# Moving the closing copies, joins and one low part at the end of each 512-token chunk

## The chip, the cores and the metric

One core of a Trainium2 chip runs the whole program in one launch. The metric is the device time of one execution in microseconds (us). In the text PE is the matmul engine, PEld its weight loads, DVE the vector engine, ACT the scalar engine, POOL GpSimd, and SP the queue that issues most DMAs. Every engine takes its instructions in the order in which the program wrote them.

## The reference

The input `x` has 4 x 3008 tokens of 256 values. The first half mixes along the sequence: a real FFT, a complex 256 x 256 product with bias, a soft threshold, and the inverse FFT. The second half is a feed-forward layer over the 12032 resulting tokens, and the change lies in it alone:

```
h = x @ w_in                                     # 256 -> 2048
g = max(h, 0) + alpha * min(h, 0)
out = g @ w_out                                  # 2048 -> 256
```

All matrices are float32. The kernel splits each operand into a rounded high part and a low rest, and a product of two operands is three matmuls: high by high, high by low, low by high.

## The kernel before, in words

Up to about 690 us the kernel does the transforms and the feed-forward layer of the first 4480 tokens. The other 7552 tokens go through it in chunks of 512 (`SC`): 14 whole ones and a last one of 384 (`NS2` is 15). This stage is the loop over `k` at the end of `fft_mix_moe`, line 1207.

The 2048 hidden values of a chunk are made in 8 **pairs** (`PR`) of two blocks of 128. One round of the loop handles pair `k`:

- `s_l1` (line 781) issues 12 matmuls of 512 columns (line 791), 6 for each of the two blocks, into PSUM tiles `ps_h`, of which there are two. For each block ACT takes the negative part (line 794) and DVE finishes the activation into `sq` (line 795). With that the `ps_h` bank is free for the next pair.
- `s_l2` (line 874) runs the second layer for the pair two rounds earlier (`SLAG` is 2), 21 matmuls of 256 columns (lines 888 to 890). It uses Strassen's scheme in Winograd's form: seven products in place of eight. The first product goes to `o_last`, the next two to a tile `c`, two to `a`, two to `b`.
- `s_sums` (line 799) makes the seven operands out of `sq`. ACT: the high part `dh` of three blocks (line 810), the high parts `h13` (821) and `h24` (824) of the sums. DVE: the sums `t13` (816) and the two halves of `t24` (818, 820), the low parts `dl` (819) and `l13` (825). POOL: the low part `l24` (826). `h24` needs the second half of `t24`, and as ACT works in order, line 794 of the next pair comes behind `h24`.

The lines of the DVE for one pair are therefore, in order, 795 twice, 816, 818, 819, 820, 825; those of ACT 794 twice, 810, 821, 824.

When the eighth pair of a chunk has gone through `s_l2`, its output lies in four PSUM pieces and must be joined. That is in the round of the second pair of the next chunk, `k` = 9, 17, ..., 113. It is called **E** here, the rounds after it E+1 to E+7, and the eight rounds from one E to the next a **period**. In E, `s_copy` (line 903) lets ACT copy four pieces into SBUF (line 909), between `h13` and `h24`. Then `s_out` (line 912) starts: it is a generator, and each `next` lets it go one step. Three joins on DVE (line 921) come at the end of E, behind `l13`; one more in each of E+1 to E+4; then `turn(1)` in E+5 and `turn(0)` in E+7, each of which transposes half of the chunk with two DVE instructions (line 927) and leaves up to 12 DMAs for the SP queue, which are issued by `put` in the round after. In E+1 the first product of the new chunk goes to `o_last`, so it needs the copy of `o_last` to be over, and the products for `a` and `b` need the copies and joins that read the old `a` and `b`.

In some rounds the loop also rebuilds 376 tokens from the transform: 16 matmuls (line 617), copies on ACT (line 654) and low parts on DVE (line 656). Of the 13 periods from the first E (`k` = 9) to the last (`k` = 113), 9 have one such group and 4 have two.

In the last chunk (`z_parts`, `z_l2`) the sums aren't formed; there the second layer is plain, and its 384 tokens are stored at the very end by lines 858 and 860 and three DMAs on SP.

The order around a chunk's end is written out by hand in these lines of the loop:

```
s_sums(*spairs[k], None if last else ends)
if ends is not None:
    ending = s_out(ends)
    next(ending)
```

Of the kernel before, what the change touches and what calls it, by code (L numbers as in the profile page):

```python
# [9 lines left out]
F32 = mybir.dt.float32  # L10
# [5 lines left out]
AF = mybir.ActivationFunctionType  # L16
ALU = mybir.AluOpType
# [76 lines left out]
def fft_mix_moe(ctx, tc, x, w_r, w_i, b_r, b_i, w_in, w_out, alpha, la, rb, lc, rd, lf, cf, sel, out):  # L94
# [25 lines left out]
    NS2 = -(-(B * S - T0) // SC)  # L120
# [4 lines left out]
    work = ctx.enter_context(tc.tile_pool(name="work", bufs=2))  # L125
# [5 lines left out]
    V, G, A, PE = nc.vector, nc.gpsimd, nc.scalar, nc.tensor  # L131

    def f(t):
        return t.bitcast(F32)
# [199 lines left out]
    def put(*queues):  # L334
        for n, (o, i) in enumerate(stores):
            (queues or (nc.sync,))[n % max(len(queues), 1)].dma_start(out=o, in_=i)
        stores.clear()
# [42 lines left out]
    pa, pb, pm, p1, pc = {}, {}, {}, {}, {}  # L380
# [296 lines left out]
    o_last = ps_o.tile([128, 2, C], F32, tag="ol", name="o_last", bufs=1)  # L677
# [62 lines left out]
    HS = SC // 2  # L740
# [36 lines left out]


    sg, sa, sq = {}, {}, {}

    def s_l1(n, t):
        yh, yl = yt[CC + n]
        w1 = SC if n < NS2 - 1 else ZC
        q = work.tile([128, 2, SC], F32, tag="xt", name="sq")[:, :, 0:w1]
        for j in range(2):
            m = 2 * t + j
            ps = ps_h.tile([128, SC], F32, tag="h", name="ps_h")[:, 0:w1]
            k = 0
            for ct in range(CT):
                for w, a in ((0, yh), (0, yl), (1, yh)):  # L790
                    PE.matmul(ps, wi_h[m // FH][:, w, ct, 128 * (m % FH):128 * (m % FH) + 128], a[:, ct, 0:w1],  # L791
                              start=(k == 0), stop=(k == 3 * CT - 1))
                    k += 1
            A.activation(out=q[:, j], in_=ps, func=AF.Relu, scale=-1.0)  # L794
            V.scalar_tensor_tensor(out=q[:, j], in0=q[:, j], scalar=beta_s[:, m:m + 1], in1=ps,  # L795
                                   op0=ALU.mult, op1=ALU.add)
        sq[n, t] = q

    def s_sums(n, t, ends=None):
        q = sq.pop((n, t))  # L800
        if n == NS2 - 1:
            z_parts(t, q)
            return
        q = q.rearrange("p j n -> p (j n)")
        b12, b11, b22, b21 = (q[:, HS * k:HS * k + HS] for k in range(4))
        dh = work.tile([128, 3 * HS], F32R, tag="Xh", name="dh")
        dl = work.tile([128, 3 * HS], F32R, tag="Xl", name="dl")
        h13 = work.tile([128, 2, HS], F32R, tag="xh", name="h13")
        l13 = work.tile([128, 2, HS], F32R, tag="Yh", name="l13")
        A.activation(out=dh, in_=q[:, HS:], func=AF.Copy)  # L810
        d = [(dh[:, HS * k:HS * k + HS], dl[:, HS * k:HS * k + HS]) for k in range(3)]
        t13 = work.tile([128, 2, HS], F32, tag="zst", name="t13", bufs=3)
        t24 = work.tile([128, 2, HS], F32, tag="bt", name="t24", bufs=3)
        h24 = work.tile([128, 2, HS], F32R, tag="xl", name="h24")
        l24 = work.tile([128, 2, HS], F32R, tag="Yl", name="l24")
        V.tensor_tensor(out=t13, in0=q[:, HS:3 * HS].rearrange("p (k n) -> p k n", k=2),  # L816
                        in1=b12.unsqueeze(1).to_broadcast([128, 2, HS]), op=ALU.subtract)
        V.tensor_tensor(out=t24[:, 0], in0=b22, in1=t13[:, 0], op=ALU.add)
        V.tensor_tensor(out=dl, in0=q[:, HS:], in1=f(dh), op=ALU.subtract)  # L819
        V.tensor_tensor(out=t24[:, 1], in0=b21, in1=t24[:, 0], op=ALU.subtract)  # L820
        A.activation(out=h13, in_=t13, func=AF.Copy)
        if ends is not None:
            s_copy(ends)
        A.activation(out=h24, in_=t24, func=AF.Copy)  # L824
        V.tensor_tensor(out=l13, in0=t13, in1=f(h13), op=ALU.subtract)
        G.tensor_tensor(out=l24, in0=t24, in1=f(h24), op=ALU.subtract)  # L826
        sg[n, t] = d + [(h[:, k], l[:, k]) for h, l in ((h13, l13), (h24, l24)) for k in range(2)]

    def z_parts(t, q):
        g = []  # L830
        for j, tags in enumerate((("xh", "Yh"), ("xl", "Yl"))):
            hi, lo = (work.tile([128, SC], F32R, tag=tag, name="zg")[:, 0:ZC] for tag in tags)
            A.activation(out=hi, in_=q[:, j], func=AF.Copy)
            (V if j else G).tensor_tensor(out=lo, in0=q[:, j], in1=f(hi), op=ALU.subtract)
            g.append((hi, lo))
        sg[NS2 - 1, t] = g
# [59 lines left out]
             (block(0, 0), b11, a[:, 0], r, False), (block(1, 0), b21, a[:, 1], False, z),  # L896
             (s4, b22, b[:, 0], r, False), (s3, t3, b[:, 1], False, z)])

    so = {}

    se = {}

    def s_copy(n):

        a, b, c = sa[n]
        se[n] = []
        for p in (a[:, 0], c[:, 1], o_last[:, 0], b[:, 0]):
            t = work.tile([128, HS], F32, tag="gl", name="se", bufs=4)
            A.activation(out=t, in_=p, func=AF.Copy)
            se[n].append(t)  # L910

    def s_out(n):

        a, b, c = sa.pop(n)
        p1, p5, p4, p3 = se.pop(n)
        u2, u3, u4 = (work.tile([128, HS], F32, tag="gh", name="su", bufs=4) for _ in range(3))
        c1 = work.tile([128, 2, HS], F32, tag="Yt", name="c1", bufs=1)
        c2 = work.tile([128, 2, HS], F32, tag="Yc", name="c2", bufs=1)

        def join(o, x, y, op=ALU.add):  # L920
            V.tensor_tensor(out=o, in0=x, in1=y, op=op)

        def turn(k):
            pool, tag = ((const, "bias"), (work, "os"))[k]
            o = pool.tile([128, HS // 32, 32, 2], F32, tag=tag, name="oT", bufs=1)
            for h, src in enumerate((c1, c2)):
                V.transpose(out=o[:, :, :, h], in_=src[:, k].rearrange("p (b c) -> p b c", c=32))
            s_store(T0 + SC * n + HS * k, o)

        join(u2, c[:, 0], p1)  # L930
        join(c1[:, 1], a[:, 1], p1)
        join(u3, b[:, 1], u2)
        yield
        join(c2[:, 1], u3, p4)
        yield
        join(u4, u2, p5, ALU.subtract)
        yield
        join(c1[:, 0], u4, p3)
        yield
        join(c2[:, 0], u3, p5, ALU.subtract)  # L940
        yield
        turn(1)
        yield
        yield
        turn(0)
        yield

    def s_store(s0, o):

        rows = out.rearrange("(b p r) c -> b p r c", b=B, r=R)  # L950
        for k in range(HS // 128):
            n, end = s0 // CH + 32 * k, s0 // CH + 32 * k + 32
            j = 0
            while n < end:
                dg, p = divmod(n, NP)
                w = min(NP - p, end - n)
                g = dg % NCH
                for ci in range(4):
                    src = o[32 * ci + j:32 * ci + j + w, 4 * k:4 * k + 4].rearrange("p i c h -> p i (c h)")
                    stores.append((rows[dg // NCH][p:p + w, CH * g:CH * g + CH, 64 * ci:64 * ci + 64], src))  # L960
                n += w
                j += w
# [33 lines left out]
    with tc.manual_schedule():  # L996
# [151 lines left out]
        spairs = [(n, t) for n in range(NS2) for t in range(PR)]  # L1148
# [33 lines left out]
        def do(when, i):  # L1182
            for fn, args in when.pop(i, ()):
                fn(*args)
# [21 lines left out]
        ending = None  # L1206
        for k in range(len(spairs) + SLAG):
            ends = None
            do(pre, k)
            if k < len(spairs):  # L1210
                s_l1(*spairs[k])
            do(post, k)
            put()
            if k < SLAG:
                l2(NS - 2 + 2 * k)
            if k == 1:
                do(todo, NS - 1)
            if k >= SLAG:
                n, t = spairs[k - SLAG]
                if n == NS2 - 1:  # L1220
                    z_l2(t)
                else:
                    s_l2(n, t)
                    ends = n if t == PR - 1 else None
            if ending is not None:
                next(ending, None)
            if k < len(spairs):
                last = spairs[k][0] == NS2 - 1
                if last and ends is not None:
                    s_copy(ends)  # L1230
                s_sums(*spairs[k], None if last else ends)
            if ends is not None:
                ending = s_out(ends)
                next(ending)
        assert not pre and not post
        put(nc.scalar, nc.sync)
        assert not todo and not mid
# [30 lines left out]
```

## Time and profile before

| | |
|---|---|
| median of 3 runs | 1353.62 us (1352.44 to 1354.51) |
| time of the profiled execution | 1354.4 us |
| its span, first to last instruction | 1352.6 us |
| PE busy | 1333.0 us, 99% |
| DVE busy | 1047.4 us, 77% |
| ACT busy | 775.7 us, 57% |
| POOL busy | 396.6 us, 29% |
| granted clock of PE | 0.999 |

A busy share is an average over the whole span. PE's matmuls are pipelined and their ends are modelled, so that a short wait of PE can be missing from its busy time; the starts of its weight loads show it. In timelines a row gives the start in us from the start of the span, the duration, the engine, the line, the operation, and what it was waiting for in square brackets. Rows that follow each other with one line and one tile are merged, with their count behind the x.

### The profile page before, as it was taken

Reading aid. Unit: us, or ns where it says so; the run is one execution under the profiler, and the core shown is the slowest. Engines: PE = TensorE matmul, PEld = TensorE weight load, DVE = VectorE, ACT = ScalarE, POOL = GpSimd, SP = SyncE. Lnnn points to the kernel's source line nnn. Section 1 sums busy time; section 2 is a strip of 40 time slices with the busy share of each in tenths; the row PEclk is TensorE's granted clock in tenths of the full one; section 3 lists DMA queues with packets and bytes.
Section 4 is the critical chain, followed back from the end, with each engine's and each line's share of the span. In section 5 each row is a group of like instructions: output and inputs, shape, how many; then the busy total and the mean of one; then the engine's idle time right before and its main releaser. Section 6 shows DMA issues by size and latency. Waiting matters only on the chain.

```text
span 1352.6 us, 25212 instructions
## 1 busy us (share of the span) xinstructions
PE 1333.0 (99%) x9158; PEld 1244.5 (92%) x9158; DVE 1047.4 (77%) x1962; ACT 775.7 (57%) x1555; POOL 396.6 (29%) x417
## 2 busy tenths in 40 slices
PE   8999999999999999999999999999999999999997
PEld 4979999999999999999999999899899888998897
DVE  2767856777777777776678888888888888888884
ACT  3566655665566645555556566656665656566653
POOL 3964742222222222222222222222221222222221
PEclk9999999999999999999999999999999999999999
DMA  9974223342333312111110011100010001000101
GB/s 234 248 199 146 80 94 105 110 135 71 98 115 110 115 50 79 55 57 40 36 36 1 11 32 26 40 12 24 23 40 14 23 20 40 17 21 20 28 17 28
DMA packets 88119, 89.66 MB, mean 66 GB/s; under 512 B 42317, under 2 KB 70448, under 8 KB 87995
## 3 DMA queue, kind: packets, MB, share of 16 engines
q1 hardware_dynamic: 79700, 77.02, 20.2%
q0 software_dynamic: 5168, 8.02, 2.3%
q10 hardware_dynamic: 3127, 3.01, 0.7%
q8 instruction: 72, 1.18, 0.4%
q14 instruction: 52, 0.43, 0.1%
HBM read 50.49 MB, written 34.34 MB: 63 GB/s over the span
## 4 chain that ended last, share of the span: by engine, by line
PE 73%; DVE 12%; issue 7%; DMA 3%; ACT 3%; POOL 1%; SPq 1%; ACTq 0%; DVEq 0%; POOLq 0%
PE ps_h L791 15%; PE ps_h L686 13%; PE ps_m L488 6%; PE ps_o L888 4%; PE ps_o L890 4%; PE ps_o L889 4%; PE ps_d L617 3%; DVE sq L795 3%; PE ps_o L725 3%; PE ps_o L724 3%; PE ps_o L723 3%; PE ps_b L428 2%; DVE t L816 2%; PE o_last L724 1%; PE o_last L725 1%
## 5 line engine op out<-in xcount | busy, mean ns | idle before, releaser
L791 PE MATMUL ps_h<-yh,w 128*128 128x512 f32 (+1 forms) x960 | 315.0, 389 | 0.0
L826 POOL TENSOR_TENSOR l<-t,h 128x512 fp32r<-128x512 f32 x112 | 145.0, 1295 | 478.9 <-ACT h L824 465.8
L795 DVE SCALAR_TENSOR_TENSOR sq<-sq,beta_s,ps_h 128x512 f32<-128x512 f32 (+1 forms) x240 | 167.5, 735 | 57.6 <-ACT sq L794 57.0
L791 PEld LDWEIGHTS ps_h<-yh,w 128*128 128x128 f32 x960 | 179.9, 188 | 32.3 <-DVE sq L795 0.2
L686 PE MATMUL ps_h<-yh,w 128*128 128x384 f32 (+1 forms) x704 | 206.8, 336 | 0.9 <-DVE q L693 0.9
L791 PE MATMUL ps_h<-yl,w 128*128 128x512 f32 (+1 forms) x480 | 185.7, 387 | 0.0
L697 ACT ACTIVATE gh<-q 128x384 fp32r<-128x384 f32 (+1 forms) x192 | 99.1, 516 | 144.5 <-DVE q L693 143.4
L693 DVE SCALAR_TENSOR_TENSOR q<-q,beta_s,ps_h 128x384 f32<-128x384 f32 (+1 forms) x192 | 115.5, 601 | 85.3 <-ACT q L692 83.8
L698 POOL TENSOR_TENSOR gl<-q,gh 128x384 fp32r<-128x384 f32 (+1 forms) x90 | 96.6, 1074 | 263.0 <-ACT gh L697 256.2
L810 ACT ACTIVATE dh<-sq 128x768 fp32r<-128x768 f32 x112 | 94.9, 848 | 118.2 <-DVE sq L795 65.3
L794 ACT ACTIVATE sq<-ps_h 128x512 f32<-128x512 f32 (+1 forms) x240 | 129.0, 585 | 9.2 <-PE ps_h L791 6.4
L686 PEld LDWEIGHTS ps_h<-yh,w 128*128 128x128 f32 x704 | 129.3, 189 | 3.8 <-issue 0.8
L824 ACT ACTIVATE h<-t 128x512 fp32r<-128x512 f32 x112 | 70.9, 633 | 107.1 <-DVE t L820 107.1
L686 PE MATMUL ps_h<-yl,w 128*128 128x384 f32 (+1 forms) x352 | 116.5, 331 | 0.0
L692 ACT ACTIVATE q<-ps_h 128x384 f32<-128x384 f32 (+1 forms) x192 | 91.7, 478 | 42.7 <-PE ps_h L686 41.2
L725 PE MATMUL ps_o<-w,gl 128*128 128x256 f32 x384 | 108.0, 281 | 1.7 <-POOL gl L698 1.7
L724 PE MATMUL ps_o<-w,gh 128*128 128x256 f32 x384 | 107.8, 281 | 0.0
L723 PE MATMUL ps_o<-w,gh 128*128 128x256 f32 x384 | 107.7, 280 | 0.0
L819 DVE TENSOR_TENSOR dl<-sq,dh 128x768 fp32r<-128x768 f32 x112 | 106.7, 953 | 0.3
L791 PEld LDWEIGHTS ps_h<-yl,w 128*128 128x128 f32 x480 | 90.2, 188 | 13.6
L888 PE MATMUL ps_o<-h,sw_a 128*128 128x256 f32 x336 | 94.2, 280 | 0.0
L890 PE MATMUL ps_o<-l,sw_a 128*128 128x256 f32 x336 | 93.0, 277 | 0.0
(195 smaller groups left out, 3590.1 us busy)
## 6 DMA issues: line engine op xcount, KB each, us to landing
zt<-zd SPq DMA_DIRECT2D x32, 384.0 KB
zd<-zst SPq DMA_DIRECT2D x37, 256.0 KB
ad<-ast SPq DMA_DIRECT2D x48, 192.0 KB
bt<-ad SPq DMA_DIRECT2D x72, 128.0 KB
xt<-in_x SPq DMA_DIRECT2D x21, 320.0 KB
out<-oT SPq DMA_DIRECT2D x152, 32.0 KB
cw_s<-in_moe_w_in SPq DMA_DIRECT2D x8, 512.0 KB
cw_s<-in_moe_w_out SPq DMA_DIRECT2D x8, 512.0 KB
```

What stands on the lines that cost most here:

```text
L686: PE.matmul(ps, wi_h[m // FH][:, w, ct, 128 * (m % FH):128 * (m % FH) + 128], a[:, ct, 0:n], start=(k == 0), stop=(k == 3 * CT - 1))
L693: V.scalar_tensor_tensor(out=q, in0=q, scalar=beta_s[:, m:m + 1], in1=ps, op0=ALU.mult, op1=ALU.add)
L723: PE.matmul(a, hi[:, t], w[:, 0], start=(i, k) in first, stop=False)
L724: PE.matmul(a, hi[:, t], w[:, 1], start=False, stop=False)
L725: PE.matmul(a, lo[:, t], w[:, 0], start=False, stop=(i, k) in last)
L791: PE.matmul(ps, wi_h[m // FH][:, w, ct, 128 * (m % FH):128 * (m % FH) + 128], a[:, ct, 0:w1], start=(k == 0), stop=(k == 3 * CT - 1))
L794: A.activation(out=q[:, j], in_=ps, func=AF.Relu, scale=-1.0)
L795: V.scalar_tensor_tensor(out=q[:, j], in0=q[:, j], scalar=beta_s[:, m:m + 1], in1=ps, op0=ALU.mult, op1=ALU.add)
L819: V.tensor_tensor(out=dl, in0=q[:, HS:], in1=f(dh), op=ALU.subtract)
L826: G.tensor_tensor(out=l24, in0=t24, in1=f(h24), op=ALU.subtract)
L888: PE.matmul(o, wh, gh, start=first, stop=False)
L890: PE.matmul(o, wh, gl, start=False, stop=last)
```

## The change

At E, two copies (`o_last` and the first half of `a`) go ahead of `dh` on ACT; two joins go between the first half of `t24` and `dl` on DVE; the other two copies go behind `h13`, and the third join goes behind `dl`, ahead of the second half of `t24`. `l13` of that pair is issued a round later, ahead of the sums of E+1. The further steps of `s_out` are: nothing in E+1, a join in E+2, `turn(1)` in E+3, a join in E+4, two joins in E+5, nothing in E+6, `turn(0)` in E+7. At the last end (`k` = 113) the four copies and three joins are issued in one go ahead of that pair's parts, the fourth join follows in the next round, `turn(1)` and three joins in the round after, `turn(0)` in the third round; before, the same steps took seven rounds.

```diff
 def s_sums(n, t, ends=None):
...
         l13 = work.tile([128, 2, HS], F32R, tag="Yh", name="l13")
+        if ends is not None:
+            next(ends)
         A.activation(out=dh, in_=q[:, HS:], func=AF.Copy)
...
         V.tensor_tensor(out=t24[:, 0], in0=b22, in1=t13[:, 0], op=ALU.add)
+        if ends is not None:
+            next(ends)
         V.tensor_tensor(out=dl, in0=q[:, HS:], in1=f(dh), op=ALU.subtract)
-        V.tensor_tensor(out=t24[:, 1], in0=b21, in1=t24[:, 0], op=ALU.subtract)
         A.activation(out=h13, in_=t13, func=AF.Copy)
         if ends is not None:
-            s_copy(ends)
+            next(ends)
+        V.tensor_tensor(out=t24[:, 1], in0=b21, in1=t24[:, 0], op=ALU.subtract)
         A.activation(out=h24, in_=t24, func=AF.Copy)
-        V.tensor_tensor(out=l13, in0=t13, in1=f(h13), op=ALU.subtract)
+
+        def low():
+            V.tensor_tensor(out=l13, in0=t13, in1=f(h13), op=ALU.subtract)
+
+        if ends is None:
+            low()
+        else:
+            waiting.append(low)
         G.tensor_tensor(out=l24, in0=t24, in1=f(h24), op=ALU.subtract)
...
 def s_out(n):
...
-        join(u2, c[:, 0], p1)
+        A.activation(out=p4, in_=o_last[:, 0], func=AF.Copy)
+        A.activation(out=p1, in_=a[:, 0], func=AF.Copy)
+        yield
         join(c1[:, 1], a[:, 1], p1)
+        join(u2, c[:, 0], p1)
+        yield
+        A.activation(out=p3, in_=b[:, 0], func=AF.Copy)
+        A.activation(out=p5, in_=c[:, 1], func=AF.Copy)
         join(u3, b[:, 1], u2)
         yield
+        if n < NS2 - 2:
+            yield
         join(c2[:, 1], u3, p4)
         yield
+        turn(1)
+        if n < NS2 - 2:
+            yield
         join(u4, u2, p5, ALU.subtract)
-        yield
+        if n < NS2 - 2:
+            yield
         join(c1[:, 0], u4, p3)
-        yield
         join(c2[:, 0], u3, p5, ALU.subtract)
         yield
-        turn(1)
-        yield
-        yield
+        if n < NS2 - 2:
+            yield
         turn(0)
         yield
...
             do(post, k)
             put()
+            while waiting:
+                waiting.pop()()
...
-            if ending is not None:
+            if ends is not None:
+                ending = s_out(ends)
+                if spairs[k][0] == NS2 - 1:
+                    for _ in range(3):
+                        next(ending)
+                    ends = None
+            elif ending is not None:
                 next(ending, None)
             if k < len(spairs):
-                last = spairs[k][0] == NS2 - 1
-                if last and ends is not None:
-                    s_copy(ends)
-                s_sums(*spairs[k], None if last else ends)
-            if ends is not None:
-                ending = s_out(ends)
-                next(ending)
+                s_sums(*spairs[k], None if ends is None else ending)
```

## Rows read from the trace of the kernel before

**Rows 1.** The page's first part: busy time and share of each engine.

```profile
PE 1333.0 (99%) x9158; PEld 1244.5 (92%) x9158; DVE 1047.4 (77%) x1962; ACT 775.7 (57%) x1555; POOL 396.6 (29%) x417
```

**Rows 2.** Waits of PE's weight loads: in total, times, longest.

```profile
PEld ps_o L888 <- DVE c L921: 3.2, 11, 0.3
...
PEld o_last L888 <- ACT se L909: 3.0, 10, 0.4
...
PEld ps_h L791 <- DVE sq L795: 0.2, 1, 0.2
```

**Rows 3.** Timeline of all engines near 1110 us: one pair, and the next start.

```profile
1108.38 1.06 ACT L794 ACTIVATE sq<-ps_h 128x512 f32<-128x512 f32 x2
...
1108.99 1.41 DVE L795 SCALAR_TENSOR_TENSOR sq<-sq,beta_s,ps_h 128x512 f32<-128x512 f32 x2 [0.64 <-ACT sq L794]
...
1109.79 0.19 PEld L791 LDWEIGHTS ps_h<-yh,w 128*128 128x128 f32 x1
...
1115.11 0.19 PEld L791 LDWEIGHTS ps_h<-yh,w 128*128 128x128 f32 x1
```

**Rows 4.** Timeline of ACT over the period from 910.27 us, line 794 alone.

```profile
913.84 1.07 ACT L794 ACTIVATE sq<-ps_h 128x512 f32<-128x512 f32 x2
...
918.96 1.06 ACT L794 ACTIVATE sq<-ps_h 128x512 f32<-128x512 f32 x2
...
924.55 1.06 ACT L794 ACTIVATE sq<-ps_h 128x512 f32<-128x512 f32 x2
...
940.52 1.06 ACT L794 ACTIVATE sq<-ps_h 128x512 f32<-128x512 f32 x2
...
946.64 1.11 ACT L794 ACTIVATE sq<-ps_h 128x512 f32<-128x512 f32 x2
...
952.35 1.07 ACT L794 ACTIVATE sq<-ps_h 128x512 f32<-128x512 f32 x2
...
957.99 1.07 ACT L794 ACTIVATE sq<-ps_h 128x512 f32<-128x512 f32 x2
```

**Rows 5.** Timeline of DVE at E, the pair whose round begins at 774.54.

```profile
780.30 0.69 DVE L816 TENSOR_TENSOR t<-sq 128x512 f32<-128x512 f32 x1
...
782.30 0.42 DVE L820 TENSOR_TENSOR t<-sq,t 128x256 f32<-128x256 f32 x1
782.64 0.69 DVE L825 TENSOR_TENSOR l<-t,h 128x512 fp32r<-128x512 f32 x1
783.24 0.42 DVE L921 TENSOR_TENSOR su<-ps_o,se 128x256 f32<-128x256 f32 x1
...
784.24 1.40 DVE L795 SCALAR_TENSOR_TENSOR sq<-sq,beta_s,ps_h 128x512 f32<-128x512 f32 x2
```

**Rows 6.** Timeline of ACT at the same E.

```profile
780.36 0.85 ACT L810 ACTIVATE dh<-sq 128x768 fp32r<-128x768 f32 x1 [1.04 <-DVE sq L795]
...
782.43 0.39 ACT L909 ACTIVATE se<-ps_o 128x256 f32<-128x256 f32 x1
782.82 0.63 ACT L824 ACTIVATE h<-t 128x512 fp32r<-128x512 f32 x1
783.35 1.07 ACT L794 ACTIVATE sq<-ps_h 128x512 f32<-128x512 f32 x2
```

**Rows 7.** Three periods: their length, then line 617's time on PE, PEld, clock.

```profile
731.03:774.54 43.51, 1.92 (x16) 1.87 (x16) 1.00 0.03 7
774.54:820.40 45.86, 3.84 (x32) 3.73 (x32) 1.00 0.12 30
820.40:864.40 44.00, 1.92 (x16) 1.87 (x16) 1.00 0.09 22
```

**Rows 8.** Timeline of all engines from 1346 us to the end.

```profile
1345.74 0.38 ACT L858 ACTIVATE zo<-ps_o 128x256 f32<-128x256 f32 x1 [1.56 <-issue]
1345.87 1.82 SPq L336 DMA_DIRECT2D out<-oT  x4
1347.79 2.02 SPq L336 DMA_DIRECT2D out<-zo  x3
```

More of the change, by code (lines that the diff above doesn't have):

```diff
@@ L779, in fft_mix_moe @@
     sg, sa, sq = {}, {}, {}
+    waiting = []
     def s_l1(n, t):
@@ L897, in s_l2 @@
              (s4, b22, b[:, 0], r, False), (s3, t3, b[:, 1], False, z)])
[L899 to L910, printed above, removed]
     def s_out(n):
         a, b, c = sa.pop(n)
-        p1, p5, p4, p3 = se.pop(n)
+        p1, p3, p4, p5 = (work.tile([128, HS], F32, tag="gl", name="se", bufs=4) for _ in range(4))
         u2, u3, u4 = (work.tile([128, HS], F32, tag="gh", name="su", bufs=4) for _ in range(3))
@@ L928, in turn @@
             s_store(T0 + SC * n + HS * k, o)
+        A.activation(out=p4, in_=o_last[:, 0], func=AF.Copy)
+        A.activation(out=p1, in_=a[:, 0], func=AF.Copy)
+        yield
+        join(c1[:, 1], a[:, 1], p1)
         join(u2, c[:, 0], p1)
-        join(c1[:, 1], a[:, 1], p1)
+        yield
+        A.activation(out=p3, in_=b[:, 0], func=AF.Copy)
+        A.activation(out=p5, in_=c[:, 1], func=AF.Copy)
         join(u3, b[:, 1], u2)
         yield
+        if n < NS2 - 2:
+            yield
         join(c2[:, 1], u3, p4)
         yield
+        turn(1)
+        if n < NS2 - 2:
+            yield
         join(u4, u2, p5, ALU.subtract)
-        yield
+        if n < NS2 - 2:
+            yield
         join(c1[:, 0], u4, p3)
-        yield
         join(c2[:, 0], u3, p5, ALU.subtract)
         yield
-        turn(1)
-        yield
-        yield
+        if n < NS2 - 2:
+            yield
         turn(0)
```

## The prediction, made before the change was run

> **What bounds the kernel now.** The page's first part comes first. The reader is to see PE busy for 99% of the span and DVE for 77% [rows 1]: there are no large holes on PE, so a change at 14 places can give or take only a per cent or so. (A measurement of this kernel can tell about 0.2%, 2.7 us, from no change.)
>
> Next the waits of PE. At chunk ends PE waits for the copy of `o_last` (3.0 us in 10 places) and for the join that reads `a` (3.2 us in 11); for the `ps_h` bank, which DVE's line 795 frees, the view has 0.2 us once [rows 2]. By this view 6.2 us are to be had and nothing else is in the way. I don't trust the 0.2, since ends of matmuls are modelled, so I go to a timeline near 1110 us. There the first `sq` begins at 1108.99; two take 1.41, so the first ends at about 1109.73, and PE's next pair begins at 1109.79. The pair after begins at 1115.11, 5.32 us later [rows 3]. Now ACT's line 794, pair to pair, in a period: 5.12, 5.59, then three times 5.32 (15.97 together), then 6.12, 5.71 and 5.64 [rows 4]. PE's 5.32 is exactly the step of ACT and DVE in a pair with one join. So here PE is paced by a **lap** of the other two engines: ACT 794, DVE 795 twice, 816, 818, 819, 820, then ACT 824, and behind it ACT 794 of the next pair.
>
> The lap closes because ACT works in order and `h24` (line 824) waits for the second half of `t24` (line 820). At E the row of line 824 starts at 782.82, 0.10 after line 820 ends at 782.72, and 794 follows 0.53 later [rows 5, 6]. The eight laps of the period sum to 44.15 us (957.99 less 913.84) [rows 4]; a period with one rebuilt group lasts 44.00 [rows 7]. That is the point of the whole reading: lap and PE are nearly equal, and whatever is put into the lap comes out as time.
>
> **The change part by part.** All of it is DVE and ACT work that exists already; what counts is whether a piece stands inside the lap or beside it.
>
> - *Joins at E.* Before, `l13` and three joins run after line 820, while ACT does `h24` and 794 of the next pair: beside the lap. They start at 782.64, and the next `sq` at 784.24; three joins take 784.24 less 783.24, 0.33 each [rows 5]. Now all three stand ahead of line 820, inside: +1.00. A rule speaks for more. The Trainium skill, VectorE: DVE Perf Modes, "The DRAIN you can't avoid", says that each operation is followed by a flush of about its duration less 266 ns; for joins of 0.42 us that would be an estimated 0.57 each, 1.7 in all, and some 5 us more over seven periods. The trace doesn't agree for these joins, at 0.33 apart; the page itself exempts operations that aren't held.
> - *Copies at E.* Two go ahead of `dh`, where ACT idles 1.04 us, and take 0.39 each at most; two fall between `h13` and `h24`, where they stand now [rows 6]. Nothing. If the idle time were gone, `dh` would be late by up to 0.8, and `dl` with it.
> - *PE's two waits* go: the copy of `o_last` can start at 779.32, where ACT falls idle, and not at about 782.4 [rows 6], and the join that reads `a` moves as far. Their worth is not added separately, since a paced PE spends the same time at line 791 instead.
> - *E+1.* Before, the first `sq` starts 0.89 after 794 (783.35 to 784.24), because joins are in front of it, against 0.61 elsewhere [rows 3, 5, 6]; 0.28 is saved. In exchange `l13` (0.60, from 782.64 to 783.24 [rows 5]) takes the place of a join of 0.33: 0.27 lost. Sum 0. `l13` is then ready at the start of E+2, and its product is read some 3 us into E+2.
> - *E+2, E+4, E+6, E+7*: the same amount as before. *E+3*: two transposes take the place of a join, +0.32 (5.64 less 5.32 [rows 4]). *E+5*: two joins take the place of the transposes, 0.
> - *DMAs.* `turn(1)`'s stores leave SP two rounds earlier, at 0.46 us each (1.82 for 4 [rows 8]), 5.5 for twelve. In SP's order they pass no load: loads of the period are issued in E+1 and E+3, ahead of them, and the next one seven rounds on. POOL's queue keeps its order; `l24` follows `h24`, a microsecond later at E, and is read two rounds later. Nothing for both.
>
> So the lap of a period grows by 1.00 + 0.32 = 1.32 us. The 7 inner periods with one group have a lap already as long as the period: 7 x 1.32 = 9.2. In the 4 with two groups PE has more of its own to do: 45.86 [rows 7], of which 0.56 are its waits at the end (6.2 over 11 [rows 2]), leaves 45.3; the lap before is about 44.15 + 1.07, the difference that a group makes in its two pairs (6.12 less 5.64 and 5.71 less 5.12 [rows 4]); after, 46.5. So 46.5 less 45.86, 0.7 each, 2.8. The first and last whole periods are shorter than the lap (43.51 against 44.15 [rows 4, 7]) and live on a lead that PE's longer rebuilt rounds left; I take 1.0 each, between 0 and 1.32, nearer the upper since 0.64 of lead is spent already: 2.0. Together +14.0.
>
> - *The last end.* Before, the last four of `turn(0)`'s stores hold SP until 1347.7, and the three final stores follow until 1349.81, though the last of them has had its data since 1346.12 [rows 8]. With those stores rounds earlier, the final one can go at 1346.12 and takes 0.67: 1346.8, a gain of 3.0. Bounds: 0, if the landing of something else ends the run, and 3.7 (the end of line 858). The bunched joins and transposes there lie on DVE in pairs that form no sums; I take nothing, bounds 0 and 1.7 (four joins, and 0.32).
>
> Sum: +14.0 less 3.0, +11.0. The profiled execution takes 1354.4, 0.8 above the median, so 1365.4 for it and 1353.6 + 11.0 = **1364.6 us** for the median.
>
> **Rivals.**
> *Faster: PE's waits go and nothing takes their place.* Then 6.2 + 3.0 are gained, 1344.4 us. For it speaks that the waits are really there [rows 2], and that DVE is 23% idle [rows 1]. By the Trainium skill, Perfetto Trace Analysis, "Identifying the Most-Contended Engine" and "Optimization Strategy", PE with the highest occupancy is the engine to optimize, by making what its gaps wait for start sooner; that rule gives this rival, and the trace bears out its gaps and not its silence on the lap. Decisive is whether a period has over 1.32 us of lead to spare; only the first begins with any I could find, and pairs 5.32 apart at a lead of 0.06 [rows 3] speak against the others. Chance 0.10.
> *No change: the lap's growth is caught up.* PE loses at E+1 about what it waited there before (0.56), and rebuilt rounds give the rest back, so that a period gains 0 to 0.3; with the tail's 3.0 that gives about 1352.6 us, and up to 1354. For it: with a group PE's round is longer by nearly two us [rows 7]. Against: that is in the 44.00 already, and equals the lap. Chance 0.06.
> *Slower, the forecast*, 0.84.
>
> **How the numbers follow.** The forecast's own bounds: lowest, 0.9 us in seven periods, nothing in the others, 3.7 at the end: +2.6, 1356.2; highest, 1.47 (45.47 less 44.00) in all 13 and nothing at the end: +19, 1372.7. The range 1355.5 to 1371.0 leaves out the faster rival, most of the other and the topmost corner. Slower by over 0.2% (above 1356.3) 0.84, within 0.2% 0.06, faster 0.10.
>
> **What would show it.** Right: both rows of PE's waits at line 888 gone; line 824 at E about 1 us later behind 816; ACT's line 794 from E to E+1 6.1 apart, E+3 to E+4 5.64; periods with one group about 45.4; the last store of SP issued with line 858's end, not 3 us behind it. Wrong: periods no longer than 44, or line 820 at E 2.0 us behind line 816 as now.

## The result, and the profile after

The changed kernel takes 1366.14 us, median of 5 runs (1365.19 to 1367.22), beside 1353.62 us for the kernel before on the same chip (5 runs, 1352.44 to 1354.51). The ratio is 1.0092, 95% interval 1.0077 to 1.0106. The profiled execution after took 1365.8 us with a span of 1364.0, against 1354.4 and 1352.6 before.

Line numbers have shifted by up to 12: line 791 is 792 now, 794 is 795, 795 is 796, 810 is 813, 816 is 819, 819 is 824, 820 is 828, 824 is 829, 825 is 832, 921 is 920, and 858 is 870. The page's first part, and the one row of PE's waits that has come up (line, what it waited for: us in total, times, longest):

```profile
PE 1340.2 (98%) x9158; PEld 1248.8 (92%) x9158; DVE 1047.8 (77%) x1962; ACT 777.4 (57%) x1555; POOL 397.2 (29%) x417
```

```profile
PEld ps_h L792 <- DVE sq L796: 16.9, 35, 0.8
```

Against [rows 1] nothing is to be seen but 7 us more of PE, whose ends are modelled. Against [rows 2] the two rows of the chunk ends (6.2 us) are gone, and the `ps_h` bank has 16.9 us in 35 places where it had 0.2 in one. That is the whole change in two lines: PE waits no longer at the chunk ends, but at the `ps_h` bank.

The two rows of before are not apart from the lap, however. PE's rows before show how the join at E (line 921, one place behind the row 783.24 of [rows 5]) held it, and where its next round then began:

```profile
784.04 0.19 PEld L888 LDWEIGHTS ps_o<-dh,w 128*128 128x128 f32 x1 [0.30 <-DVE c L921]
...
785.46 0.19 PEld L791 LDWEIGHTS ps_h<-yh,w 128*128 128x128 f32 x1
```

The round E+2 begins here 785.46 - 784.24 = 1.22 us behind the start of line 795 of E+1 [rows 5]. In 11 of the 13 periods before, this distance is 1.22 or 1.23. In the changed kernel it is 0.80 in all but the first, as long as from line 795 to PE in [rows 3]. So before, the lap held PE once in a period, through the copies and joins, and now it holds PE through the bank.

Now the periods, from one E to the next, by the view of windows as in [rows 7] (length, then line 617's time on PE and PEld, granted clock, DMA share, GB/s). First comes the first period, then one with two groups and one with one group. The last whole period and the sum of all 13 close the list:

```profile
730.27:774.25 43.98, 1.92 (x16) 1.87 (x16) 1.00 0.03 7
774.25:821.44 47.19, 3.84 (x32) 3.73 (x32) 1.00 0.12 29
...
913.64:959.03 45.39, 1.92 (x16) 1.87 (x16) 1.00 0.09 21
...
1279.81:1324.35 44.54, 1.92 (x16) 1.87 (x16) 1.00 0.09 21
sum 594.08, PE 32.63 PEld 31.72; mean PE 2.51 PEld 2.44
```

Each span can be cut at the first E and at the last, where the periods start and stop. What the edits do is in the second and third columns:

| kernel | to the first E | 13 periods | last E to the end | span |
|---|---|---|---|---|
| before | 731.03 | 578.82 | 42.76 | 1352.6 |
| after | 730.27 | 594.08 | 39.67 | 1364.0 |
| difference | -0.76 | +15.26 | -3.09 | +11.4 |

The first column is the same code in both kernels. It moves by itself, as the last section tells.

Where the lap grew is seen at E. DVE's timeline, the E that answers to [rows 5]:

```profile
780.67 0.69 DVE L819 TENSOR_TENSOR t<-sq 128x512 f32<-128x512 f32 x1
781.47 0.43 DVE L821 TENSOR_TENSOR t<-sq,t 128x256 f32<-128x256 f32 x1
781.81 0.42 DVE L920 TENSOR_TENSOR c<-ps_o,se 128x256 f32<-128x256 f32 x1
782.14 0.41 DVE L920 TENSOR_TENSOR su<-ps_o,se 128x256 f32<-128x256 f32 x1
782.48 0.95 DVE L824 TENSOR_TENSOR dl<-sq,dh 128x768 fp32r<-128x768 f32 x1
783.34 0.42 DVE L920 TENSOR_TENSOR su<-ps_o,su 128x256 f32<-128x256 f32 x1
783.67 0.41 DVE L828 TENSOR_TENSOR t<-sq,t 128x256 f32<-128x256 f32 x1
```

ACT's timeline of the same E, answering to [rows 6]:

```profile
779.57 0.39 ACT L929 ACTIVATE se<-o_last 128x256 f32<-128x256 f32 x1
779.83 0.40 ACT L930 ACTIVATE se<-ps_o 128x256 f32<-128x256 f32 x1
780.73 0.85 ACT L813 ACTIVATE dh<-sq 128x768 fp32r<-128x768 f32 x1 [0.50 <-DVE sq L796]
...
784.18 0.63 ACT L829 ACTIVATE h<-t 128x512 fp32r<-128x512 f32 x1 [1.21 <-DVE t L828]
784.72 1.07 ACT L795 ACTIVATE sq<-ps_h 128x512 f32<-128x512 f32 x2
```

PEld's timeline, the two starts of PE that follow:

```profile
786.14 0.19 PEld L792 LDWEIGHTS ps_h<-yh,w 128*128 128x128 f32 x1 [0.81 <-DVE sq L796]
...
791.72 0.19 PEld L792 LDWEIGHTS ps_h<-yh,w 128*128 128x128 f32 x1 [0.27 <-DVE sq L796]
```

The two copies sit in ACT's idle time and `dh` keeps its place, 0.06 behind the start of line 819, as before behind line 816 [rows 5, 6]. The three joins (line 920) push the second half of `t24` (line 828) back. `h24` then starts 784.18 - 780.67 = 3.51 us behind line 819, where it was 782.82 - 780.30 = 2.52 [rows 5, 6]: +0.99. ACT's next line 795 stands in order behind it, DVE's line 796 waits for that, and PE waits 0.81 for the bank which line 796 frees.

### The profile page after: what moved, and what is told of

The parts are those of the page before. It is cut to its first block, busy times and chain, and to the rows that moved or that the text cites. A ratio compares the mean times of both kernels' runs of the same rounds, so it can differ in the third digit from the quotient of the medians.

```text
span 1364.0 us, 25198 instructions
## 1 busy us (share of the span) xinstructions
PE 1340.2 (98%) x9158; PEld 1248.8 (92%) x9158; DVE 1047.8 (77%) x1962; ACT 777.4 (57%) x1555; POOL 397.2 (29%) x417
## 4 chain that ended last, share of the span: by engine, by line
PE 54%; DVE 22%; issue 12%; ACT 6%; DMA 4%; SPq 1%; POOL 0%; ACTq 0%; DVEq 0%; POOLq 0%
PE ps_h L686 13%; DVE sq L796 7%; PE ps_h L792 7%; PE ps_m L488 6%; DVE t L819 4%; ACT sq L795 4%; PE ps_o L725 3%; PE ps_o L724 3%; PE ps_o L723 3%; DVE t L828 3%; PE ps_b L428 2%; PE ps_d L617 2%; PE o_last L724 1%; PE o_last L725 1%; PE o_last L723 1%
## 5 line engine op out<-in xcount | busy, mean ns | idle before, releaser
L792 PE MATMUL ps_h<-yh,w 128*128 128x512 f32 (+1 forms) x960 | 320.1, 394 | 9.9 <-DVE sq L796 8.2
L792 PEld LDWEIGHTS ps_h<-yh,w 128*128 128x128 f32 x960 | 179.9, 188 | 50.0 <-DVE sq L796 16.9
```

## The experiments

Seven kernels were run: two alone, each with one part of the change (e1, e3), one with the short low part moved alone (e6), two that take part of the change back (e2, e7), and two that cut the lap (e4, e8). Rows carry the line numbers of their own kernel: 888 is 890 in e3 and 896 in e6, the copy of line 909 is 917 in e6 and 916 in e8, and in e4 794 is 796, 820 is 831 and 824 is 834. e1 to e4 share the runs of the kernel before (median 1354.02 us, 25 runs), and so do e6 to e8 (1354.15 us, 13 runs). The columns are those of the table above.

| kernel | median us | ratio to before (95%) | to the first E | 13 periods | last E to the end |
|---|---|---|---|---|---|
| e1, last end alone | 1351.95 | 0.9984 (0.9974, 0.9993) | 729.93 | 578.68 | 39.72 |
| e2, after, three joins back | 1355.04 | 1.0005 (0.9995, 1.0014) | 731.97 | 581.30 | 39.63 |
| e3, copies early alone | 1354.56 | 1.0002 (0.9992, 1.0012) | 730.62 | 578.47 | 43.16 |
| e4, after, lap cut | 1344.21 | 0.9929 (0.9912, 0.9945) | 730.60 | 572.26 | 39.65 |
| e6, `l13` late alone | 1356.42 | 1.0019 (1.0010, 1.0029) | 729.67 | 581.07 | 42.84 |
| e7, after, third join back | 1362.54 | 1.0061 (1.0045, 1.0076) | 729.20 | 589.72 | 39.66 |
| e8, before, lap cut, new last end | 1344.74 | 0.9928 (0.9913, 0.9943) | 729.86 | 572.26 | 39.74 |

**The last end alone (e1).** The kernel before, with only the steps of the last end bunched:

```diff
 def s_out(n):
...
+        if n == NS2 - 2:
+            turn(1)
         join(u4, u2, p5, ALU.subtract)
-        yield
+        if n < NS2 - 2:
+            yield
         join(c1[:, 0], u4, p3)
-        yield
+        if n < NS2 - 2:
+            yield
         join(c2[:, 0], u3, p5, ALU.subtract)
         yield
-        turn(1)
-        yield
-        yield
+        if n < NS2 - 2:
+            turn(1)
+            yield
+            yield
         turn(0)
```

> Before, with the last end's steps bunched as in the change and nothing else. Lap theory: the pairs of the chunks are untouched, the three final stores on SP no longer stand behind the transposed ones, 3.0 us less, about 1350.6; SP's last store begins within 0.2 us of the end of line 858's second copy. Rival (the landing of something else, or DVE's bunched joins in the last chunk, decide the end): no gain, 1353.6, or up to 1.7 us of loss.

Periods as before (578.68 against 578.82), and 39.72 us from the last E to the end, 3.04 less. The median moved by 2.1, a ratio of 0.9984, where 3.0 was expected; the ten executions lie between 1349.94 and 1353.31. The timeline of the last microseconds shows why:

```profile
1342.97 2.55 SPq L336 DMA_DIRECT2D out<-zo  x3
...
1344.56 0.38 ACT L858 ACTIVATE zo<-ps_o 128x256 f32<-128x256 f32 x1 [1.61 <-issue]
```

The last of the three final stores begins at 1344.96, 0.02 behind the end of the copy whose data it takes (1344.56 + 0.38 = 1344.94), and ends at 1342.97 + 2.55 = 1345.52, 0.58 behind it. In [rows 8] the same distance is 1349.81 - 1346.12 = 3.69. The last end's gain is thus its own, and it comes from SP's queue.

**The joins taken out of the lap again (e2).** The changed kernel, with its three joins behind `h24`:

```diff
 def s_sums(n, t, ends=None):
...
-        if ends is not None:
-            next(ends)
         V.tensor_tensor(out=dl, in0=q[:, HS:], in1=f(dh), op=ALU.subtract)
...
         A.activation(out=h24, in_=t24, func=AF.Copy)
+        if ends is not None:
+            next(ends)
...
 def s_out(n):
...
-        join(c1[:, 1], a[:, 1], p1)
-        join(u2, c[:, 0], p1)
-        yield
         A.activation(out=p3, in_=b[:, 0], func=AF.Copy)
         A.activation(out=p5, in_=c[:, 1], func=AF.Copy)
+        yield
+        join(c1[:, 1], a[:, 1], p1)
+        join(u2, c[:, 0], p1)
         join(u3, b[:, 1], u2)
```

> The change, with its three joins at E put back behind the second half of t24 (copies early, l13 a round later and the new spacing of the later steps stay). Lap theory: the lap at E falls from 6.12 to 5.12 us, only E+3's 0.32 stays in the lap, periods with one group near 44.4, about 1352 us with the 3.0 of the tail. Rival (the late l13, the early transposes or the moved copies make the change slow, not where the joins stand): stays above 1360.

12.8 of the 15.3 us are gone. The seven inner periods with one group average 44.52 us, against 45.51 in the changed kernel: 1.00 less each, three joins of 0.33. Two of the periods, and what is left of the wait:

```profile
775.48:821.25 45.77, 3.84 (x32) 3.73 (x32) 1.00 0.12 30
821.25:865.86 44.61, 1.92 (x16) 1.87 (x16) 1.00 0.09 22
```

```profile
PEld ps_h L792 <- DVE sq L796: 5.3, 21, 0.7
```

The lap of E is 5.11 again, and that of E+3 stays at 5.64. The periods sum to 2.5 us more than before. The seven with one group are 0.46 longer each (44.52 against 44.06), of which ACT's laps show 0.35 (44.50 against 44.15), the E+3 turn's 0.32 for the most part; the four with two groups are 0.2 shorter. PE's two rows at line 888 are gone here too: the rounds E+1, which took 73.51 us in the 13 periods before, take 68.02, close to the 67.77 of the kernels with the lap cut. These 5.5 us were gained there and lost again in the other rounds. The median is 3 us over what was expected; the periods grew by 2.5 where the expected time leaves them 1.4 (1352 less 1353.6, and the 3.0 of the end), and another 0.94 stands in the first column, in code that was not touched. The rest is left open.

**The third join alone taken out (e7).** A dose in between. The changed kernel, only `u3`'s join behind `h24`:

```diff
 def s_sums(n, t, ends=None):
...
         A.activation(out=h24, in_=t24, func=AF.Copy)
+        if ends is not None:
+            next(ends)
...
 def s_out(n):
...
         A.activation(out=p5, in_=c[:, 1], func=AF.Copy)
+        yield
         join(u3, b[:, 1], u2)
...
-                    for _ in range(3):
+                    for _ in range(4):
                         next(ending)
```

> The change, with the third join alone behind the second half of t24, so that two joins and not three stand inside the lap at E. Lap theory: the lap at E is 5.79 us, a period 0.33 shorter than the change's, 4.3 us over 13 periods, about 1362 us: two thirds of the way from the kernel with the joins put back. Rival (one particular join, the one that waits for the copies or for u2, makes E late): all or nothing, 1355 or 1366.

```profile
819.70:864.93 45.23, 1.92 (x16) 1.87 (x16) 1.00 0.09 21
```

```profile
PEld ps_h L792 <- DVE sq L796: 13.0, 35, 0.7
```

The windows and the waits again: periods with one group average 45.18, 0.33 under the changed kernel's 45.51, one join's worth. E's lap is 5.77, between 5.11 and 6.10. So the time follows the joins one by one, as the lap has it: 44.52 with none inside, 45.18 with two, 45.51 with three.

**The copies early, and nothing else (e3).** This gives PE what the change was to give it, without anything in the lap:

```diff
 def s_sums(n, t, ends=None):
...
+        if ends is not None:
+            s_copy(ends, 0)
         A.activation(out=dh, in_=q[:, HS:], func=AF.Copy)
...
-            s_copy(ends)
+            s_copy(ends, 1)
         A.activation(out=h24, in_=t24, func=AF.Copy)
...
-    def s_copy(n):
+    def s_copy(n, part):
...
-        for p in (a[:, 0], c[:, 1], o_last[:, 0], b[:, 0]):
+        for p in ((o_last[:, 0], a[:, 0]), (b[:, 0], c[:, 1]))[part]:
...
 def s_out(n):
...
-        join(u2, c[:, 0], p1)
         join(c1[:, 1], a[:, 1], p1)
+        join(u2, c[:, 0], p1)
```

> Before, with the copies of o_last and a's first half ahead of dh, and the join of a first of the three; nothing else. Lap theory: PE's waits at line 888 fall from 6.2 us to under 2, but the periods with one group stay at 44.0, as PE then waits at line 791; only the four periods with two groups and the last gain, some 0.4 each, about 1351.6 us. Rival (PE's gaps are what is to be had): their 5 to 6 us are gained, about 1348.

What PE still waits for at the chunk ends, and the two periods:

```profile
PEld ps_o L890 <- issue: 2.1, 9, 0.3
```

```profile
774.14:819.84 45.70, 3.84 (x32) 3.73 (x32) 1.00 0.12 30
819.84:863.84 44.00, 1.92 (x16) 1.87 (x16) 1.00 0.09 22
```

By the view, the 6.2 us of [rows 2] have become 2.1. By the starts of PE's rounds less is gone: the 13 rounds E+1 take 71.47 us where they took 73.51, 2.04 less, and the other rounds 1.69 more, so that the periods are shorter by 0.35 in all. The end is 0.40 longer, and the ratio is 1.0002. Where the time went shows in the round E+4 of the period of [rows 4], first before, then here (PE's start of E+4, DVE's line 795 of that round, PE's start of E+5):

```profile
931.50 0.19 PEld L791 LDWEIGHTS ps_h<-yh,w 128*128 128x128 f32 x1
...
935.81 1.41 DVE L795 SCALAR_TENSOR_TENSOR sq<-sq,beta_s,ps_h 128x512 f32<-128x512 f32 x2 [0.64 <-ACT sq L794]
...
936.71 0.19 PEld L791 LDWEIGHTS ps_h<-yh,w 128*128 128x128 f32 x1
```

```profile
930.71 0.19 PEld L791 LDWEIGHTS ps_h<-yh,w 128*128 128x128 f32 x1
...
935.23 1.41 DVE L795 SCALAR_TENSOR_TENSOR sq<-sq,beta_s,ps_h 128x512 f32<-128x512 f32 x2 [0.64 <-ACT sq L794]
...
936.03 0.19 PEld L791 LDWEIGHTS ps_h<-yh,w 128*128 128x128 f32 x1
```

Before, PE's round is its own 5.21 and the next begins 0.90 behind line 795. Here it is 5.32, the lap, and the next begins 0.80 behind, the distance of [rows 3] at which PE waits for the bank. PE comes sooner, to a bank that is not free. One thing blurs this run: the new order of the first two joins made the lap of E+1 5.71 in place of 5.59, which may have cost up to 0.1 in a period. In e2 that lap is 5.59, so e2 is the cleaner case. The expectation had 0.4 in each period with two groups; they gained 0.1.

**The short low part a pair later, alone (e6).**

```diff
 def s_sums(n, t, ends=None):
...
-        V.tensor_tensor(out=l13, in0=t13, in1=f(h13), op=ALU.subtract)
+
+        def low():
+            V.tensor_tensor(out=l13, in0=t13, in1=f(h13), op=ALU.subtract)
+
+        if ends is None:
+            low()
+        else:
+            waiting.append(low)
...
             put()
+            while waiting:
+                waiting.pop()()
```

> Before, with l13 of E's pair issued a round later and nothing else. Lap theory: at E+1 l13 adds 0.60 to the lap and takes 0.28 of delay of sq away, 5.59 becomes 5.9, a period grows by 0.32 as in the kernel with the joins put back: some 2.5 us over the periods, about 1356.3 us, although the joins come 0.6 us earlier. Rival (PE's gaps count): the wait for the join that reads a goes, 3 us less, about 1350.6.

```profile
PEld ps_h L792 <- DVE sq L796: 3.5, 12, 0.3
PEld o_last L896 <- ACT se L917: 3.4, 10, 0.4
```

`l13` brings its 0.60 us [rows 5] into the lap of E+1 and saves the 0.28 by which `sq` was late there, so 0.32 should be added. That lap goes from 5.59 to 5.92, by 0.33, and the periods grow by 2.25 us in all, those with one group from 44.06 to 44.31. In the full change E+1 loses a join, and its lap stays at 5.59. The wait of PE for the join that reads `a` has gone here too, and again without a gain.

**The lap cut (e4, e8).** If the lap is what counts, then taking `h24` out of the way of ACT's next line 795 must give more than the change cost. In e4, the changed kernel, `h24` and `l24` of every pair go behind the first half of the next pair's lines 795 and 796:

```diff
 def s_l1(...):
...
             V.scalar_tensor_tensor(out=q[:, j], in0=q[:, j], scalar=beta_s[:, m:m + 1], in1=ps,
                                    op0=ALU.mult, op1=ALU.add)
+            while late:
+                late.pop()()
...
 def s_sums(n, t, ends=None):
...
-        A.activation(out=h24, in_=t24, func=AF.Copy)
+
+        def high():
+            A.activation(out=h24, in_=t24, func=AF.Copy)
+            G.tensor_tensor(out=l24, in0=t24, in1=f(h24), op=ALU.subtract)
+
+        late.append(high)
...
-        G.tensor_tensor(out=l24, in0=t24, in1=f(h24), op=ALU.subtract)
```

> The change, with h24 and l24 of every pair issued behind the first line 794 of the next pair, so that the lap is cut at the place where ACT's order closes it. Lap theory: the joins ahead of the second half of t24 cost nothing any more, periods of 43.5 and 45.3 us, about 1345 us (6 us of PE's waits and 3.0 of the tail gone). Rival (the joins cost DVE or PSUM time in themselves, or h24 is then late for its product): stays above 1358.

The second and third period, and ACT's timeline at E:

```profile
774.11:819.43 45.32, 3.84 (x32) 3.73 (x32) 1.00 0.13 30
819.43:862.95 43.52, 1.92 (x16) 1.87 (x16) 1.00 0.09 22
```

```profile
781.07 0.60 ACT L796 ACTIVATE sq<-ps_h 128x512 f32<-128x512 f32 x1
782.08 0.63 ACT L834 ACTIVATE h<-t 128x512 fp32r<-128x512 f32 x1 [0.42 <-DVE t L831]
```

`h24` still waits for `t24`, but the next pair's first `sq` no longer stands behind it. Every inner period with one group is 43.51 or 43.52 and every one with two 45.32, PE's rows for the `ps_h` bank of these pairs are gone, and the kernel takes 1344.21 us. It beats both kernels.

e8 does the same to the kernel before, with e1's last end and with the copies, joins and `l13` where they were before; its edit is the sum of the two above.

> Before, with the last end bunched and h24 and l24 behind the first line 794 of the next pair; copies, joins and l13 stand where they stood before. Lap theory: the copies and joins at E come earlier by themselves, as DVE and ACT run ahead of PE, so PE's waits at line 888 go without being aimed at: periods of 43.5 and 45.3, about 1344.5 us, like the change with the lap cut. Rival (with the lap cut the change's moves are what removes PE's waits): the waits stay, some 6 us more, about 1350.

```profile
773.38:818.70 45.32, 3.84 (x32) 3.73 (x32) 1.00 0.12 30
```

```profile
780.23 0.39 ACT L916 ACTIVATE se<-o_last 128x256 f32<-128x256 f32 x1
```

The sum of the periods is that of e4, 572.26 us, 6.42 less than in e1. Of these 6.42, 5.61 lie in the rounds E+1, where PE's two waits were. So with the lap cut the change's moves at E are worth nothing either way. The copy of `o_last` comes 780.23 - 773.38 = 6.85 us after E's start without having been moved, where before it came 782.17 - 774.54 = 7.63 after (line 909's row for `o_last`), and no row of PE's waits names it any more.

## Why the prediction was right

The forecast was slower, 1364.6 us; it is 1366.14, inside 1355.5 to 1371.0. By its own steps:

- *The lap as the bound*: shown. One-group periods follow the joins inside the lap in steps of 0.33 (e2, e7), a shorter lap gives PE's own 43.51 (e4, e8), and taking PE's two waits away without shortening the lap gives nothing (e2) or next to nothing (e3). Cut at the start of E+2, where the lap lets PE go, the seven one-group periods average 44.15 us before and 45.49 after, and ACT's laps of the same periods 44.15 and 45.49. In one point the reading was too simple: 5.32 in [rows 3] is not PE's pace in every round. Before, most rounds from E+2 to E+4 are PE's own 5.21, and the lap takes the difference back in E+1 by PE's two waits.
- *The lap closes through `h24`*: the row chosen for it doesn't show it alone, as ACT's last copy ends at 782.82 too [rows 6]. The row of line 829 in the changed kernel does (1.21 us of waiting for `t24`), and so do e4 and e8.
- *Joins at E, +1.00*: 0.99 at `h24`. ACT's line 795 goes from 5.12 to 6.10 apart, as this timeline of the changed kernel's ACT shows for the period of [rows 4]:

```profile
917.51 1.07 ACT L795 ACTIVATE sq<-ps_h 128x512 f32<-128x512 f32 x2
...
923.61 1.07 ACT L795 ACTIVATE sq<-ps_h 128x512 f32<-128x512 f32 x2
...
929.20 1.07 ACT L795 ACTIVATE sq<-ps_h 128x512 f32<-128x512 f32 x2
...
934.52 1.07 ACT L795 ACTIVATE sq<-ps_h 128x512 f32<-128x512 f32 x2
...
940.16 1.07 ACT L795 ACTIVATE sq<-ps_h 128x512 f32<-128x512 f32 x2
...
962.97 1.07 ACT L795 ACTIVATE sq<-ps_h 128x512 f32<-128x512 f32 x2
```

  The rule of the Trainium skill, VectorE: DVE Perf Modes, "The DRAIN you can't avoid", would have made it 1.7, by the estimate in the prediction, which reads it without the exemption of operations that aren't held. The joins stand 0.33 to 0.34 apart here (781.81, 782.14, 782.48), so the trace still disagrees with it for them.
- *E+1 and E+5 nothing, E+3 +0.32*: E+1 is 5.59 before and after, and E+3 is 5.64 (940.16 - 934.52). E+5 is 6.14 where it was 6.12. The eight laps sum to 45.46 us (962.97 - 917.51) where they were 44.15: +1.31, predicted +1.32.
- *Copies and DMAs nothing*: in e4, which has both as the change puts them, a period is as long as in e8, which has neither. So neither costs anything there. In e2, where both stand as in the change and the lap is not cut, the laps grow by 0.35 with 0.32 of it E+3's, so under the lap they cost next to nothing too.
- *PE's two waits*: gone as predicted, and their time spent again at `ps_h`.
- *The sum of the periods, +14.0*: 15.3. This is the term that was mis-sized, and by parts: seven periods with one group +10.2 (predicted 9.2), four with two groups +3.5 (2.8), the first and last +1.6 (2.0). In the seven, a period grew by 1.45 where the lap grew by 1.34. Cut at E, they averaged 44.06 before, a little under their lap of 44.15, as PE began them with some lead left from the rebuilt rounds; after, 45.51, a little over 45.49. The term took lap and period to be equal already (44.15 and 44.00) and left this out.
- *Two groups*: that the +2.8 came as near as it did was luck. It took the lap before to be 45.2, below PE's own work and waits, and to grow by 1.32. ACT's laps of these periods average 45.71 before and 46.64 after, +0.93. So the lap bounded them before too, as e3 also says: its periods of this kind are still 45.72 on average where PE's own are 45.32 (e4). The two errors nearly cancel: 46.5 was predicted for the lap after, 46.64 measured.
- *First and last*: the first period had a lead to spare and paid only 0.47 of the 1.0, and the second paid for it: 47.19 less 45.86 is 1.33, where 0.7 was predicted, while the other three with two groups grew by 0.73 on average. The last grew by 1.1.
- *The last end, -3.0*: -3.09, and -3.04 alone in e1. The bunched joins and transposes there show no cost, as taken: all kernels with the new last end need 39.63 to 39.74 us for it. The final stores end 0.6 us behind the copy, where 0.67 was predicted:

```profile
1358.65 2.56 SPq L336 DMA_DIRECT2D out<-zo  x3
...
1360.24 0.38 ACT L870 ACTIVATE zo<-ps_o 128x256 f32<-128x256 f32 x1 [1.62 <-issue]
```

- *The faster rival* (1344.4 us, PE's gaps go and nothing takes their place) falls by e2, where PE's two waits are gone and the periods are as long as the lap, and less sharply by e3. By the rule behind it, the Trainium skill, Perfetto Trace Analysis, "Identifying the Most-Contended Engine" and "Optimization Strategy", what PE's gaps wait for is to be made to start sooner. In this trace that alone was no gain: 5.5 us of PE's rounds E+1 went in e2, and the periods grew by 2.5. The time itself, 1344.2, was reached by e4 over another way.
- *The no-change rival* falls by the periods: nothing is caught up, 45.51 against 44.06.

Against the median the forecast is 1.5 us low. The periods explain 1.3, the end takes back 0.1, and the rest is within what one run differs from the next.

## What to carry to other kernels

Where two helper engines and the busiest one work in a ring through in-order queues, measure the ring: the distance between two instances of the same helper instruction, round by round, against the busiest engine's own round. If they are equal, whatever is put into the ring comes out as time, however idle its engines look (DVE 77%, ACT 57%), and a wait of the busy engine may be the ring's even where it is named after something else; taken away there, it comes up at another place. Look instead for the one instruction that makes an early operation of the next round stand behind a late one of this round, and let the two change places: that took 6.4 us off the periods here, where three joins in the wrong place put 12.8 on.

## What was not expected of the hardware

- A wait view can name the bound by other names: before, the row for the `ps_h` bank has 0.2 us and the two rows at line 888 have 6.2 [rows 2]. Cutting the lap, which touches neither the copies nor the joins, took 6.4 us off the same periods (578.68 in e1, 572.26 in e8), 5.6 of it where those two rows lie.
- A join that reads the result of the one directly ahead of it starts later. DVE's timeline of e2 at E has it 0.51 behind; the one before it, which reads nothing of its neighbour's, 0.34. It is the same in the other 12 periods to 0.01 us:

```profile
783.82 0.42 DVE L920 TENSOR_TENSOR c<-ps_o,se 128x256 f32<-128x256 f32 x1
784.16 0.41 DVE L920 TENSOR_TENSOR su<-ps_o,se 128x256 f32<-128x256 f32 x1
784.67 0.42 DVE L920 TENSOR_TENSOR su<-ps_o,su 128x256 f32<-128x256 f32 x1
```

  In e3, where the same two joins come next to each other, it is 0.45. In the kernel before another join stands between the two, and the steps are 0.33 to 0.34 in 12 of 13 periods; in the changed kernel `dl` stands between them. Why e2 has 0.07 more than e3 is open.
- The granted clock stays at 1.00 in every period shown, with PE waiting up to 0.81 us at a time.
- The first E begins between 729.20 and 731.97 us in the nine kernels, though in seven of them, these two among them, no edit reaches the code ahead of it (in e4 and e8 `h24` moves from the first pair on). That is 0.2% of the time, as much as a small change here is worth, and the reason to compare the periods and not the spans.
